# Decode attention on one core: one exp with eight masked copies, a product over half of K, and a whole third-last load

## The chip, the cores and the metric

One of the eight cores of a Trainium2 chip runs the whole kernel; the other cores are idle. The metric is the time of one execution on the device in microseconds, as a median of several runs. A sentence on names: PE is the matmul engine, DVE the vector engine, ACT the scalar engine, and SP the engine that only issues loads here.

Some words for reading the profiles. A page is the profiler's summary of one profiled run. A line of a timeline gives start and length in microseconds, engine, line of the kernel, operation, what it writes and reads, and how many instructions it sums up; brackets at its end give the time that the engine stood idle before it and what ended that. In a line of groups the numbers after the bar are busy microseconds and mean nanoseconds of one, then idle time before the group and what ended it. The granted clock is the share of PE's full speed that the trace's record of the clock gives for a stretch (1.0 or 0.5 in the profiles of both kernels). Slack is how much later a load could be issued without making the run longer.

## The reference

```python
B, H, Sq, Skv, Dh = 8, 32, 1, 4096, 128      # all bf16
def reference(q, k, v):
    scale = q.shape[-1] ** -0.5
    scores = jnp.einsum('bhqd,bhkd->bhqk', q, k) * scale
    attn = softmax(scores, axis=-1)
    return jnp.einsum('bhqk,bhkd->bhqd', attn, v)
```

There are 256 heads with one query each. K and V are 268 MB each and every byte is used once, so this is a kernel that streams memory.

## The kernel before

Eight heads make a tile: 128 partitions, 16 to a head, with 256 keys of 128 values on each partition. A tile of K or of V is one load of 8.39 MB. There are 32 tiles and three buffers of that size, which K and V share in turn.

DVE multiplies K by q and folds the 128 products of a key to 64 or 32; PE adds up further by multiplying with the identity; DVE finishes the sums to scores. One maximum per head follows, then ACT takes the exp. Eight copies of the weights are wanted, one per head, each nonzero only on that head's 16 partitions, since each value matmul takes the weights of all 128 partitions at once (`128*32` in the profile's lines):

```python
def product(t, lo, hi):
    kt = loads["k", t]
    qb = qbs[t]
    for c0 in range(lo, hi, MC):                     # MC = 64 keys, a quarter tile
        part = kt[:, c0 : c0 + MC, :]
        nc.vector.tensor_tensor(out=part, in0=part, in1=qb[:].to_broadcast([P, MC, D]), op=ALU.mult)
        nc.vector.tensor_tensor(out=part[:, :, 0 : D // 2], in0=part[:, :, 0 : D // 2],
                                in1=part[:, :, D // 2 : D], op=ALU.add)
        ...                                          # a second fold in some quarters
def weights_of(t):
    ...                                              # maximum of each head -> nmax
    nc.vector.tensor_scalar(out=bias[:], in0=own[:], scalar1=nmax[:, 0:1], ...)   # -1e30 for other heads
    for g in range(G):                               # G = 8
        nc.scalar.activation(out=w[:, :, g, :], in_=sc_g, func=ACT.Exp, bias=bias[:, g : g + 1],
                             scale=scale, accum_out=esum[:, t % R, g : g + 1])
```

The order of one turn, for the turns t = 1 to 29, in which a hardware loop does the value matmuls of tile t - 1:

```python
product(t, 0, Q);      sum_over_d(t, 0)              # Q = a quarter of the keys
...                                                  # result of tile t-2, q of tile t+2
product(t, Q, 2 * Q);  sum_over_d(t, 1);  scores_of(t, 0)
product(t, 2 * Q, 3 * Q);  sum_over_d(t, 2);  scores_of(t, 1)
...
product(t, 3 * Q, C);  sum_over_d(t, 3);  scores_of(t, 2)
values_loop(t - 1)                                   # 64 matmuls on PE
load("k", t + 1)                                     # waits for the value loop of tile t-2 to free its buffer
load("v", t)                                         # waits for PE's last sums of K of tile t
scores_of(t, 3);  weights_of(t);  ...
```

After the last tile PE does the values of tile 31 as the pieces of the last V come in: 32 matmuls on the first half, 30 on the later pieces, eight small ones for the last keys; then a copy, four matmuls, a scaling and the store.

Of the kernel before, what the change touches and what calls it, by code (L numbers as in the profile page):

```python
# [7 lines left out]
ACT = mybir.ActivationFunctionType  # L8
ALU = mybir.AluOpType
AX = mybir.AxisListType  # L10
BF16 = mybir.dt.bfloat16
F32 = mybir.dt.float32

G = 8
SLOTS = 3
TG = 4
R = 2
# [8 lines left out]
def kernel(  # L26
# [7 lines left out]
    nc = tc.nc  # L34
    B, H, Sq, D = q.shape
    S = k.shape[2]
    P = nc.NUM_PARTITIONS
    assert Sq == 1 and D == 128
    NH = B * H
    PH = P // G  # L40
    C = S // PH
    NT = NH // G
    scale = float(D) ** -0.5
    UC = 64
    DS = 512 // UC
    NU = C // UC
    MC = UC
    CB = 4
    RG = R * G
    NQ = NT // R  # L50
# [12 lines left out]
    consts = ctx.enter_context(tc.tile_pool(name="consts", bufs=1))  # L63
    q_pool = ctx.enter_context(tc.tile_pool(name="q_pool", bufs=3))
    w_pool = ctx.enter_context(tc.tile_pool(name="w_pool", bufs=2))
    sc_pool = ctx.enter_context(tc.tile_pool(name="sc_pool", bufs=2))
    small = ctx.enter_context(tc.tile_pool(name="small", bufs=2))
    o_pool = ctx.enter_context(tc.tile_pool(name="o_pool", bufs=1))
    ps_s = ctx.enter_context(tc.tile_pool(name="ps_s", bufs=3, space=bass.MemoryType.PSUM))
# [10 lines left out]
        out=ident[:], in_=ident[:], pattern=[[-1, P]], compare_op=ALU.not_equal,  # L80
        fill=1.0, base=0, channel_multiplier=1,
# [5 lines left out]
        out=heads[:], in_=heads[:], pattern=[[-1, G], [0, PH]], compare_op=ALU.not_equal,  # L87
        fill=1.0, base=0, channel_multiplier=1,
    )

    own = consts.tile([P, G], F32, name="own")
    nc.gpsimd.memset(own[:], 0.0)
    nc.gpsimd.affine_select(
        out=own[:], in_=own[:], pattern=[[-PH, G]], compare_op=ALU.is_ge,
        fill=NEG, base=0, channel_multiplier=1,
    )
    nc.gpsimd.affine_select(
        out=own[:], in_=own[:], pattern=[[PH, G]], compare_op=ALU.is_ge,
        fill=NEG, base=PH - 1, channel_multiplier=-1,
# [4 lines left out]
        out=same[:].rearrange("p (h x) -> p h x", x=PH),  # L104
        in_=own[:].rearrange("p (b h) -> p h b", h=TB // PH)
# [7 lines left out]
    for j in range(TG):  # L113
        part = pick[j * AG : (j + 1) * AG, :, :, :]
        nc.gpsimd.affine_select(
            out=part, in_=part, pattern=[[-1, CB], [CB * G, R], [-CB, RG]],
            compare_op=ALU.not_equal, fill=1.0, base=0, channel_multiplier=1,
        )
    ones = consts.tile([P, 1], F32, name="ones")
    nc.vector.memset(ones[:], 1.0)  # L120

    w_last = consts.tile([P, LAST, RG], BF16, name="w_last")
    nc.gpsimd.memset(w_last[:], 0.0)
# [4 lines left out]
    def behind_loop(made):  # L128
# [8 lines left out]

    cuts = {
        ("k", 0): [C // 4, C // 4, C // 2],
        ("k", NT - 3): [C // 2] * 2,  # L140
        ("k", NT - 2): [C // 2] * 2,
        ("k", NT - 1): [C // 4, C // 4, C // 2],
        ("v", NT - 1): [C // 2, C // 4, C // 8, C // 16, C // 32, LAST // 2, LAST // 2],
# [31 lines left out]
    def width_of(t, u):  # L175


        return D // 4 if u >= NU // 2 and 0 < t < NT - 3 else D // 2

    def product(t, lo, hi):  # L180
        kt = loads["k", t]
        qb = qbs[t]
        for c0 in range(lo, hi, MC):
            part = kt[:, c0 : c0 + MC, :]
            nc.vector.tensor_tensor(  # L185
                out=part, in0=part, in1=qb[:].to_broadcast([P, MC, D]), op=ALU.mult
            )
            nc.vector.tensor_tensor(  # L188
                out=part[:, :, 0 : D // 2], in0=part[:, :, 0 : D // 2],
                in1=part[:, :, D // 2 : D], op=ALU.add,  # L190
            )
            if width_of(t, c0 // UC) < D // 2:
                nc.vector.tensor_tensor(  # L193
                    out=part[:, :, 0 : D // 4], in0=part[:, :, 0 : D // 4],
                    in1=part[:, :, D // 4 : D // 2], op=ALU.add,
                )

    sums = {}

    def sum_over_d(t, u):  # L200
        kt = loads["k", t]
        ps = ps_s.tile([P, UC, DS], F32, name="ps", tag="ps")
        n = width_of(t, u) // DS
        for s in range(n):
            nc.tensor.matmul(  # L205
                ps[:], lhsT=ident[:],
                rhs=kt[:, u * UC : (u + 1) * UC, s * DS : (s + 1) * DS],
                start=(s == 0), stop=(s == n - 1),
            )
        sums[t, u] = ps  # L210
# [3 lines left out]
    def scores_of(t, u):  # L214
        if u == 0:
            scs[t] = sc_pool.tile([P, C], F32, name="sc", tag="sc")
        made = nc.vector.tensor_reduce(  # L217
            out=scs[t][:, u * UC : (u + 1) * UC], in_=sums.pop((t, u))[:], axis=AX.X, op=ALU.add
        )
        if u == NU - 1:  # L220
            behind_loop(made)

    ws = {}
    esums = {}

    def weights_of(t):
        sc = scs.pop(t)
        pmax = small.tile([P, 1], F32, name="pmax", tag="pmax")
        nc.vector.tensor_reduce(out=pmax[:], in_=sc[:], axis=AX.X, op=ALU.max)  # L229
        spread = small.tile([P, TB], F32, name="spread", tag="spread")  # L230
        nc.vector.tensor_scalar(
            out=spread[:], in0=same[:], scalar1=pmax[:, 0:1], scalar2=-scale,
            op0=ALU.add, op1=ALU.mult,
        )
        nmax = small.tile([P, 1], F32, name="nmax", tag="nmax")
        nc.vector.tensor_reduce(
            out=nmax[:], in_=spread[:], axis=AX.X, op=ALU.min, apply_transpose=True
        )
        bias = small.tile([P, G], F32, name="bias", tag="bias")
        nc.vector.tensor_scalar(  # L240
            out=bias[:], in0=own[:], scalar1=nmax[:, 0:1], scalar2=None, op0=ALU.add
        )
        w = w_pool.tile([P, C // CB, G, CB], BF16, name="w", tag="w")
        if t % R == 0:
            esums[t // R] = small.tile([P, R, G], F32, name="esum", tag="esum")
        esum = esums[t // R]
        sc_g = sc[:].rearrange("p (i m) -> p i m", m=CB)
        for g in range(G):
            nc.scalar.activation(  # L249
                out=w[:, :, g, :], in_=sc_g, func=ACT.Exp, bias=bias[:, g : g + 1], scale=scale,  # L250
                accum_out=esum[:, t % R, g : g + 1],
            )
        ws[t] = w
        if t == NT - 1:
            for i in range(LAST // CB):
                nc.gpsimd.tensor_copy(
                    out=w_last[:, i * CB : (i + 1) * CB, RG - G : RG].rearrange("p m g -> p g m"),
                    in_=w[:, (C - LAST) // CB + i, :, :],
                )
# [66 lines left out]

    def norm_of(n):
        zp = ps_z.tile([RG, 1], F32, name="zp", tag="zp")
        nc.tensor.matmul(
            zp[:], lhsT=esums.pop(n).rearrange("p r g -> p (r g)"), rhs=ones[:],  # L330
            start=True, stop=True,
        )
        zps[n] = zp

    def recip_of(n):
# [46 lines left out]
    Q = C // 4  # L382
# [3 lines left out]
    with tc.manual_schedule(engines={E.PE, E.DVE, E.Activation, E.SP}):  # L386
        q_prep(0)
        q_prep(1)
        for t in range(NT):
            loop = 0 < t <= LT  # L390
            v_last = t >= NT - 2
            n = t // R - 1
            if not loop:
                if t + 1 < NT:
                    load("k", t + 1)
                load("v", t)
            product(t, 0, Q)
            sum_over_d(t, 0)
            if 0 < t - 1 <= LT:
                if (t - 1) % R == 0:  # L400
                    norm_of(n)
                if t > 1:
                    result_of(t - 2)
            if t + 2 < NT:
                q_prep(t + 2)
            product(t, Q, 2 * Q)
            sum_over_d(t, 1)
            scores_of(t, 0)
            product(t, 2 * Q, 3 * Q)
            sum_over_d(t, 2)  # L410
            scores_of(t, 1)
            if t > 2 and t % R == 1:
                recip_of(n)
            product(t, 3 * Q, C)
            sum_over_d(t, 3)
            scores_of(t, 2)
            if loop:
                values_loop(t - 1)
                load("k", t + 1)
                load("v", t)  # L420
            if v_last:
                values_of(t - 1, 0, C)
            scores_of(t, 3)
            weights_of(t)
            if t > 2 and t % R == 1:
                finish_of(n)
            if t > 0:
                copy_of(t - 1)
                if t > 2 and t % R == 1:
                    store_of(n)  # L430
                if not loop:
                    if t % R == 0:
                        norm_of(n)
                    result_of(t - 1)
        values_of(NT - 1, 0, C // 2)
        norm_of(NQ - 1)
        recip_of(NQ - 1)
        values_of(NT - 1, C // 2, C - LAST)
        copy_of(NT - 1)
        result_of(NT - 1)  # L440
        finish_of(NQ - 1)
        store_of(NQ - 1)
# [30 lines left out]
```

## Time and profile before

| | before |
|---|---|
| time, median of 3 runs | 1252.86 us (1252.73 to 1252.98) |
| span in the profile | 1250.9 us |
| read from memory | 536.94 MB, 429 GB/s over the span |
| busy: PE, DVE, ACT | 62%, 83%, 14% |
| mean granted clock of PE | 0.787 |

The two things to look for are the throughput of the transfers, slice by slice, and what the last piece of work waited for. The prediction shows both. The row of PE's clock belongs beside them, as will turn out; here it is with the busy tenths of PE, from part 2 of the page of the kernel before, 40 slices of 31 us each:

```profile
PE   3465567755577555775557755577655776557756
PEclk9977788777887778877778777788777887778867
```

The clock granted to PE is not constant: 0.9 of full speed or more in two slices, 0.6 to 0.8 in the other 38.

### The profile page before, as it was taken

What the parts mean: (1) busy time and instruction counts of PE and PEld (TensorE: products, weight loads), DVE (VectorE), ACT (ScalarE), POOL (GpSimd) and SP (SyncE); (2) the same over time, 40 slices, a digit from 0 to 9 for tenths busy, and PEclk for the clock granted to TensorE, in tenths of its full rate; (3) what the DMA queues carried; (4) which work ended last, traced back from release to release, by engine and by line L of the source; (5) the groups of instructions that cost most, each with busy time, mean ns of one, the idle gap of its engine ahead of it and who ended that gap; (6) DMA issues with size and microseconds to landing.
All of it is one profiled execution on the core that took longest, in us unless ns stands there. A gap on an engine that the chain in (4) does not pass through costs nothing. (4 is left out here: it accounts for less than half of the span.)

```text
span 1250.9 us, 11080 instructions
## 1 busy us (share of the span) xinstructions
PE 770.4 (62%) x3078; PEld 289.4 (23%) x3078; DVE 1036.1 (83%) x586; ACT 170.7 (14%) x625; POOL 3.5 (0%) x19
## 2 busy tenths in 40 slices
PE   3465567755577555775557755577655776557756
PEld 1122122211222212222122221122221222122222
DVE  7887988888978889887798888988889887898783
ACT  0111011111011110111101111011110111101111
POOL 0000000000000000000000000000000000000000
PEclk9977788777887778877778777788777887778867
DMA  9999999999999999999999999999999999999997
GB/s 404 436 436 435 436 436 432 434 436 434 434 424 430 434 434 436 425 434 434 436 436 434 434 434 430 436 428 434 434 430 424 432 437 436 428 428 428 430 445 324
DMA packets 11577, 537.33 MB, mean 430 GB/s; under 512 B 1824, under 2 KB 2080, under 8 KB 2336
## 3 DMA queue, kind: packets, MB, share of 16 engines
q1 hardware_dynamic: 11216, 536.94, 99.4%
q8 instruction: 14, 0.23, 0.1%
q10 hardware_dynamic: 336, 0.07, 0.0%
q14 instruction: 11, 0.09, 0.0%
HBM read 536.94 MB, written 0.07 MB: 429 GB/s over the span
## 5 line engine op out<-in xcount | busy, mean ns | idle before, releaser
L185 DVE TENSOR_TENSOR kt<-kt,qb 128x8192 bf16<-128x8192 bf16 x128 | 565.3, 4416 | 127.9 <-DMA kt<-in_k_dram 103.5
L205 PE MATMUL ps<-kt,ident 128*128 128x512 bf16 x800 | 265.3, 483 | 432.4 <-DVE kt L193 366.8
L289 PE MATMUL av<-vt,w 128*32 x1740 | 426.1, 399 | 3.8
L188 DVE TENSOR_TENSOR kt<-kt 128x4096 bf16<-128x4096 bf16 x128 | 293.4, 2292 | 4.4
L289 PEld LDWEIGHTS av<-vt,w 128*32 x1740 | 174.4, 100 | 261.2 <-issue 114.4
L205 PEld LDWEIGHTS <-ident 128*128 128x128 bf16 x800 | 87.2, 113 | 597.0 <-issue 550.7
L249 ACT ACTIVATE w<-sc,bias 128x256 bf16<-128x256 f32 x256 | 126.3, 494 | 671.6 <-DVE bias L240 671.6
L217 DVE TENSOR_REDUCE sc<-ps 128x64 f32<-128x512 f32 x128 | 87.8, 686 | 57.3 <-PE ps L205 57.3
L193 DVE TENSOR_TENSOR kt<-kt 128x2048 bf16<-128x2048 bf16 x56 | 68.6, 1225 | 1.9
L345 ACT ACTIVATE comb<-av 32x512 bf16<-32x512 f32 (+1 forms) x32 | 18.8, 586 | 321.6 <-PEq L279 313.5
L275 PE MATMUL av<-vt,w 128*32 128x512 bf16 x116 | 47.1, 498 | 14.6 <-issue 13.4
L249 ACT ACTIVATION_READ_ACCUMULATOR w<-sc,bias 128x1 f32 x256 | 47.7, 187 | 0.0
L275 PEld LDWEIGHTS av<-vt,w 128*32 128x32 bf16 x116 | 6.9, 100 | 55.2 <-issue 55.2
L168 ACT ACTIVATE qg<-qh 8x128 bf16<-8x128 f32 x32 | 8.5, 267 | 73.8 <-PE qh L164 73.8
L317 PE MATMUL av<-vt,w 128*32 128x512 bf16 x190 | 14.7, 411 | 1.6 <-DMA vt<-in_v_dram 1.6
L361 PE MATMUL op<-comb,pick 32*16 32x128 bf16 (+1 forms) x128 | 12.3, 215 | 5.1 <-ACT comb L345 5.0
L229 DVE TENSOR_REDUCE pmax<-sc 128x1 f32<-128x256 f32 x32 | 13.4, 420 | 1.1
L170 PE MATMUL qp<-qg,heads 8*128 8x128 bf16 x32 | 6.9, 216 | 11.4 <-ACT qg L168 11.4
L164 PE MATMUL qh<-q_all,ident 128*8 128x128 bf16 x32 | 7.1, 223 | 8.7 <-DMA q_all<-in_q_dram 8.4
L172 ACT ACTIVATE qb<-qp 128x128 bf16<-128x128 f32 x32 | 8.9, 278 | 9.7 <-PE qp L170 9.7
L361 PEld LDWEIGHTS <-pick 32*16 32x16 bf16 (+1 forms) x128 | 6.8, 84 | 12.4 <-issue 12.0
L317 PEld LDWEIGHTS <-w 128*32 128x32 bf16 x190 | 6.5, 103 | 9.9 <-issue 5.5
(29 smaller groups left out, 47.4 us busy)
## 6 DMA issues: line engine op xcount, KB each, us to landing
kt<-in_k_dram SPq DMA_DIRECT2D x6, 4096.0 KB, 24.2
kt<-in_k_dram SPq DMA_DIRECT2D x4, 2048.0 KB, 13.4
vt<-in_v_dram SPq DMA_DIRECT2D x1, 4096.0 KB, 34.6
vt<-in_v_dram SPq DMA_DIRECT2D x1, 2048.0 KB, 39.1
vt<-in_v_dram SPq DMA_DIRECT2D x1, 1024.0 KB, 41.1
vt<-in_v_dram SPq DMA_DIRECT2D x1, 512.0 KB, 41.9
vt<-in_v_dram SPq DMA_DIRECT2D x31, 25.6
kt<-in_k_dram SPq DMA_DIRECT2D x28, 28.1
```

The source lines that it names most:

```text
L185: nc.vector.tensor_tensor(out=part, in0=part, in1=qb[:].to_broadcast([P, MC, D]), op=ALU.mult)
L188: nc.vector.tensor_tensor(out=part[:, :, 0 : D // 2], in0=part[:, :, 0 : D // 2], in1=part[:, :, D // 2 : D], op=ALU.add,)
L193: nc.vector.tensor_tensor(out=part[:, :, 0 : D // 4], in0=part[:, :, 0 : D // 4], in1=part[:, :, D // 4 : D // 2], op=ALU.add,)
L205: nc.tensor.matmul(ps[:], lhsT=ident[:], rhs=kt[:, u * UC : (u + 1) * UC, s * DS : (s + 1) * DS], start=(s == 0), stop=(s == n - 1),)
L217: made = nc.vector.tensor_reduce(out=scs[t][:, u * UC : (u + 1) * UC], in_=sums.pop((t, u))[:], axis=AX.X, op=ALU.add)
L229: nc.vector.tensor_reduce(out=pmax[:], in_=sc[:], axis=AX.X, op=ALU.max)
L249: nc.scalar.activation(out=w[:, :, g, :], in_=sc_g, func=ACT.Exp, bias=bias[:, g : g + 1], scale=scale, accum_out=esum[:, t % R, g : g + 1],)
L275: pe.matmul(av, lhsT=wf[:, i * nw : (i + 1) * nw], rhs=vf[:, i * nv : (i + 1) * nv], **how)
L289: pe.matmul(av, lhsT=wf[:, bass.ds(ow + i * nw, nw)], rhs=vf[:, bass.ds(ov + i * nv, nv)], start=False, stop=False,)
L317: nc.tensor.matmul(avs[t][j * AG : (j + 1) * AG, :], lhsT=w[:, i, :, :], rhs=vt[:, c0 : c0 + CB, :], start=(i < TG), stop=(j not in group[ ...
L345: nc.scalar.activation(out=comb[0:n, :, :], in_=av[0:n, :, :], func=ACT.Copy)
L361: nc.tensor.matmul(ops[n][:], lhsT=pick[0:e, m, r, :], rhs=comb[0:e, m, :], start=(r == 0 and m == 0), stop=(r == R - 1 and m == CB - 1),)
```

## The change

The change looks meant to save work on ACT and DVE. One exp per tile gives the weights once, and eight copies, each multiplied by a mask that is 1 on one head's partitions, spread them. In the turns 1 to 29 the first two quarters of K are multiplied in one instruction. The third-last K comes in one load instead of two. The diff is cut: the scores' buffers also go from two to one, together with the one exp.

```diff
+    mine = consts.tile([P, R, RG], F32, name="mine")      # 1 where partition and head belong together
...
-        ("k", NT - 3): [C // 2] * 2,
...
-        for c0 in range(lo, hi, MC):
-            part = kt[:, c0 : c0 + MC, :]
+        part = kt[:, lo:hi, :]
...
-        bias = small.tile([P, G], F32, name="bias", tag="bias")
-        nc.vector.tensor_scalar(out=bias[:], in0=own[:], scalar1=nmax[:, 0:1], scalar2=None, op0=ALU.add)
+        e = o_pool.tile([P, C], BF16, name="e", tag="e")
+        nc.scalar.activation(out=e[:], in_=sc[:], func=ACT.Exp, bias=nmax[:, 0:1], scale=scale,
+                             accum_out=esums[t // R][:, t % R : t % R + 1])
         for g in range(G):
             nc.scalar.activation(
-                out=w[:, :, g, :], in_=sc_g, func=ACT.Exp, bias=bias[:, g : g + 1], scale=scale,
-                accum_out=esum[:, t % R, g : g + 1],
+                out=w[:, :, g, :], in_=e_g, func=ACT.Copy, scale=mine[:, 0, g : g + 1]
             )
...
-            product(t, 0, Q)
-            sum_over_d(t, 0)
+            product(t, 0, 2 * Q if loop else Q)
+            if not loop:
+                sum_over_d(t, 0)
...                                                    # in turns 1 to 29: sums 0 and 1 together,
...                                                    # scores 0 and 1 together after the third quarter
```

The normalisation changes with it. Before, each of the eight copies brought its own sum of weights, and one matmul for a pair of tiles added them up. Now there is one sum per partition and tile, and two small matmuls with the mask add them up by head.

More of the change, by code (lines that the diff above doesn't have):

```diff
@@ L46 @@
     NU = C // UC
-    MC = UC
     CB = 4
@@ L65 @@
     w_pool = ctx.enter_context(tc.tile_pool(name="w_pool", bufs=2))
-    sc_pool = ctx.enter_context(tc.tile_pool(name="sc_pool", bufs=2))
+    sc_pool = ctx.enter_context(tc.tile_pool(name="sc_pool", bufs=1))
     small = ctx.enter_context(tc.tile_pool(name="small", bufs=2))
@@ L118 @@
         )
-    ones = consts.tile([P, 1], F32, name="ones")
-    nc.vector.memset(ones[:], 1.0)
+    mine = consts.tile([P, R, RG], F32, name="mine")
+    nc.gpsimd.memset(mine[:], 1.0)
+    nc.gpsimd.affine_select(
+        out=mine[:], in_=mine[:], pattern=[[PH * G, R], [-PH, RG]], compare_op=ALU.is_ge,
+        fill=0.0, base=0, channel_multiplier=1,
+    )
+    nc.gpsimd.affine_select(
+        out=mine[:], in_=mine[:], pattern=[[-PH * G, R], [PH, RG]], compare_op=ALU.is_ge,
+        fill=0.0, base=PH - 1, channel_multiplier=-1,
+    )
     w_last = consts.tile([P, LAST, RG], BF16, name="w_last")
@@ L182, in product @@
         qb = qbs[t]
-        for c0 in range(lo, hi, MC):
-            part = kt[:, c0 : c0 + MC, :]
+        part = kt[:, lo:hi, :]
+        nc.vector.tensor_tensor(
+            out=part, in0=part, in1=qb[:].to_broadcast([P, hi - lo, D]), op=ALU.mult
+        )
+        nc.vector.tensor_tensor(
+            out=part[:, :, 0 : D // 2], in0=part[:, :, 0 : D // 2],
+            in1=part[:, :, D // 2 : D], op=ALU.add,
+        )
+        if width_of(t, lo // UC) < D // 2:
             nc.vector.tensor_tensor(
-                out=part, in0=part, in1=qb[:].to_broadcast([P, MC, D]), op=ALU.mult
-            )
-            nc.vector.tensor_tensor(
-                out=part[:, :, 0 : D // 2], in0=part[:, :, 0 : D // 2],
-                in1=part[:, :, D // 2 : D], op=ALU.add,
-            )
-            if width_of(t, c0 // UC) < D // 2:
-                nc.vector.tensor_tensor(
-                    out=part[:, :, 0 : D // 4], in0=part[:, :, 0 : D // 4],
-                    in1=part[:, :, D // 4 : D // 2], op=ALU.add,
-                )
+                out=part[:, :, 0 : D // 4], in0=part[:, :, 0 : D // 4],
+                in1=part[:, :, D // 4 : D // 2], op=ALU.add,
+            )
     sums = {}
@@ L238, in weights_of @@
         )
-        bias = small.tile([P, G], F32, name="bias", tag="bias")
-        nc.vector.tensor_scalar(
-            out=bias[:], in0=own[:], scalar1=nmax[:, 0:1], scalar2=None, op0=ALU.add
+        if t % R == 0:
+            esums[t // R] = small.tile([P, R], F32, name="esum", tag="esum")
+        e = o_pool.tile([P, C], BF16, name="e", tag="e")
+        nc.scalar.activation(
+            out=e[:], in_=sc[:], func=ACT.Exp, bias=nmax[:, 0:1], scale=scale,
+            accum_out=esums[t // R][:, t % R : t % R + 1],
         )
         w = w_pool.tile([P, C // CB, G, CB], BF16, name="w", tag="w")
-        if t % R == 0:
-            esums[t // R] = small.tile([P, R, G], F32, name="esum", tag="esum")
-        esum = esums[t // R]
-        sc_g = sc[:].rearrange("p (i m) -> p i m", m=CB)
+        e_g = e[:].rearrange("p (i m) -> p i m", m=CB)
         for g in range(G):
             nc.scalar.activation(
-                out=w[:, :, g, :], in_=sc_g, func=ACT.Exp, bias=bias[:, g : g + 1], scale=scale,
-                accum_out=esum[:, t % R, g : g + 1],
+                out=w[:, :, g, :], in_=e_g, func=ACT.Copy, scale=mine[:, 0, g : g + 1]
             )
@@ L328, in norm_of @@
         zp = ps_z.tile([RG, 1], F32, name="zp", tag="zp")
-        nc.tensor.matmul(
-            zp[:], lhsT=esums.pop(n).rearrange("p r g -> p (r g)"), rhs=ones[:],
-            start=True, stop=True,
-        )
+        esum = esums.pop(n)
+        for r in range(R):
+            nc.tensor.matmul(
+                zp[:], lhsT=mine[:, r, :], rhs=esum[:, r : r + 1], start=(r == 0), stop=(r == R - 1)
+            )
         zps[n] = zp
@@ L405 @@
                 q_prep(t + 2)
-            product(t, Q, 2 * Q)
+            if loop:
+                sum_over_d(t, 0)
+            else:
+                product(t, Q, 2 * Q)
             sum_over_d(t, 1)
-            scores_of(t, 0)
+            if not loop:
+                scores_of(t, 0)
             product(t, 2 * Q, 3 * Q)
             sum_over_d(t, 2)
+            if loop:
+                scores_of(t, 0)
             scores_of(t, 1)
```

## The prediction

> **What bounds the kernel now.** I read the page's busy line first, then its row of DMA throughput, then the chain that ended last, then the queue of loads (times of issue and of landing), and last the timeline of one tile.
>
> The page, parts 1 to 3:
>
> ```profile
> PE 770.4 (62%) x3078; PEld 289.4 (23%) x3078; DVE 1036.1 (83%) x586; ACT 170.7 (14%) x625; POOL 3.5 (0%) x19
> ...
> DMA  9999999999999999999999999999999999999997
> GB/s 404 436 436 435 436 436 432 434 436 434 434 424 430 434 434 436 425 434 434 436 436 434 434 434 430 436 428 434 434 430 424 432 437 436 428 428 428 430 445 324
> ...
> HBM read 536.94 MB, written 0.07 MB: 429 GB/s over the span
> ```
>
> No compute engine is full; the transfers are, in every slice but the first and the last. No slice of the middle falls below 424 or stays above 436 GB/s. At 436 the 536.94 MB take 1231.5 us; the span is 1250.9, so everything that isn't transfer at that rate is 19.4 us, 1.6%. A change that leaves the bytes alone cannot gain 2% (25 us) here.
>
> The chain of work that ended last:
>
> ```profile
> DMA 3%; DVE 1%; PE 1%; SPq 0%; ACT 0%; issue 0%; DVEq 0%; ACTq 0%
> ...
> 1204.53 41.99 DMA vt<-in_v_dram
> 1246.53 0.04 issue
> 1246.57 0.41 PE av L317 x2
> ```
>
> The chain is cut short at the left, but its end is clear: the last pieces of the last V were issued at 1204.53 and landed 42 us later, because two other loads stood before them. After the landing come two matmuls, a copy, four matmuls, a scaling and the store: some 4.4 us to 1250.9.
>
> Whether the queue of loads ever runs dry is read from part 6 of the page and from the timeline of the issuing engine:
>
> ```profile
> vt<-in_v_dram SPq DMA_DIRECT2D x31, 25.6
> kt<-in_k_dram SPq DMA_DIRECT2D x28, 28.1
> ...
> 441.52 0.33 SPq L151 DMA_DIRECT2D kt<-in_k_dram  x1
> 463.58 0.33 SPq L151 DMA_DIRECT2D vt<-in_v_dram  x1
> 480.53 0.33 SPq L151 DMA_DIRECT2D kt<-in_k_dram  x1
> ```
>
> A whole load is 8.39 MB and takes 19.2 us at 436 GB/s. V lands 25.6 us after issue and K 28.1. Take off the moving and 1.3 us of fixed latency (the 4 KB store at the end landed in 1.3), and a V load has stood in the queue for 5.1 us, a K load for 7.6. So each could be issued that much later before the transfers would notice. Issues come 38.7 us apart for a pair, two times 19.2 and a little.
>
> The vector engine waits for K, not the other way round (timeline of one tile):
>
> ```profile
> 463.98 1.04 PE L275 MATMUL av<-vt,w 128*32 128x512 bf16 x2 [0.43 <-issue]
> ...
> 469.75 4.43 DVE L185 TENSOR_TENSOR kt<-kt,qb 128x8192 bf16<-128x8192 bf16 x1 [4.23 <-DMA kt<-in_k_dram]
> ...
> 474.21 2.29 DVE L188 TENSOR_TENSOR kt<-kt 128x4096 bf16<-128x4096 bf16 x1
> ...
> 476.43 4.42 DVE L185 TENSOR_TENSOR kt<-kt,qb 128x8192 bf16<-128x8192 bf16 x1
> ```
>
> DVE starts the tile when K has landed, after 4.23 us of waiting, and 32.4 us later (502.15) the sums are out and the next V is issued. DVE's spare time per tile is thus about 4.3 of 38.7 us. The value loop starts at 463.98 and its end at 480.4 lets the K load go.
>
> [...] 8192 elements 4416 ns, 4096 elements 2292, 2048 elements 1225, thus 0.52 ns an element and 150 to 160 ns fixed. [...]
>
> **The change part by part.** The name speaks of six value matmuls per loop turn, but the loop constant is 6 in both kernels; nothing changes there. The bytes stay the same.
>
> *One exp, eight copies.* Out go 256 exps (126.3 us busy), 256 accumulator reads (47.7) and 32 bias additions on DVE (7.4 us). In come 32 exps (32 x 0.494 = 15.8), 32 reads (6.0) and 256 copies with a pointer scale[...]. ACT busy falls to about 145 us. Per tile, the time from maximum to finished weights: before, eight steps of 0.49 (465.56, 466.06, 466.55), 4.0 us in all. After: the exp, its read and a wait for its output, 0.7[...]. The weights of tile t are used only a tile later, so this lies beside other work except in the last tile. The normalisation gets one more tiny accumulating matmul per pair of tiles, 16 times some 0.2 us on PE, off the path.
>
> *Two quarters in one product.* In the 29 loop tiles two multiplications of 8192 become one of 16384: 8.53 + 0.15 = 8.7 instead of 8.83 us, and the addition likewise 4.42 instead of 4.58. Saved: 0.15 twice, 0.3 us a tile. The first score reduction (0.68) moves behind the third quarter; its length stays. So the last sums, hence V's issue, come 0.3 us earlier relative to K's landing. DVE busy falls by 29 x 0.3 + 7.4 = 16 us, to about 1020, and its wait for K grows by 0.5 us a tile. The first 16 sum matmuls start after both quarters, about 13.1 us after landing (say 482.8) instead of at the loop's end (480.5). PE waits there, and has nothing that sets an end.
>
> *Third-last K whole.* Before, DVE began tile 29 at 1126.21, on the first half. Whole, it starts by the rhythm: 1091.92 + 38.7 = 1130.6, or 4.4 us later. But before, DVE then stood 3.65 us at the first score reduction, until PE had left the value loop; with the reduction moved, that wait goes. After: 1130.6 + 13.05 (both quarters) + 6.7 + 1.3 (two reductions) + 0.1 + 6.7 + 3.6 (last sums) = 1162.0, against V's issue at 1161.59. The shift is +0.4 us, against 5 of slack. Tiles 30 and 31 keep their order and are shifted by 0.2 to 0.4. The last weights are ready at 1238.3 instead of 1238.05; PE then still waits for V (1.09 us at 1242.24, 0.2 before the last two matmuls), so the shift is swallowed.
>
> Sum on the path: start of transfers 0, transfers 0 [...], tail after the last landing 0. The result is **1252.6 us**, 0.3 below the median of before.
>
> **Rivals.** *A dry queue:* the shift in tile 29 exceeds the slack, or V1 at the start is issued too late (75.42, where K2's transfer ends near 79). For it: the slack is smallest there. Against it: the shift is 0.4, and V1 moves earlier by 0.3. If I missed the removed wait, 4.4 us of shift would still be inside 5.1; a spill would make 1253 to 1256. *Faster transfers:* pairs take 38.8 us, not 38.5 as at 436 GB/s; if that loss came from the engines' traffic in SBUF, fewer instructions could give back part of 19 us, thus 1245 to 1250. Against it: stretches of 38.7 us each, tile after tile, read 429 to 434 GB/s (one 426), whatever the tile does, and I find no dip that belongs to an engine's work. *ACT as a bound:* with copies twice as dear as I think, weights come 4 us later; loop tiles have over 30 us to spare, but in the last tile half of V is waiting and PE would take the place of the landing; 1254 to 1256. *A slower clock on PE:* the loop takes 16.4 us and ends 7.6 before K's queue is dry, so even 25% would pass.
>
> **Range and chances.** The three runs of before lie within 0.25 us, and nothing on the path is touched, so I take 1251.2 to 1254.0 for 8 in 10: a little for small changes in how transfers meet, and for the tail. Faster by 2% would need more than the ceiling allows: 0.01. Slower by 2% needs a dry queue in nearly every tile: 0.01. Within 2%: 0.98.
>
> **What would show it right or wrong.** Right: the row of GB/s still at 434, landing times about 25.9 and 28, DVE busy near 1020, ACT near 145, the product of 16384 at 8.7 us, no wait for the first score in tile 29, the chain again ending in V's landing. Wrong: a slice of GB/s under 420 in the middle or near tile 29, landing times near 20.5, copies at 0.9 us, or a last chain that runs through ACT's copies instead of the landing.

The sum on the path came to 0 + 0 + 0, so 1252.6 us. ACT's 145 us came from 170.7 - 126.3 - 47.7 + 15.8 + 6.0 + 126: the 126 stands for 256 copies at 0.49 us each, my estimate, by which a copy takes as long as an exp (494 ns on the page). The time from maximum to weights came to 0.7 + 3.3 = 4.0 us after the change, thus no change, less 0.23 for the bias addition; the 3.3 for eight copies (seven steps of 0.40 and a last 0.49), an estimate too, is cut with the sum. In the trace of the kernel before, 0.40 us pass from the start of an exp to the start of its read (466.06 to 466.46). The times for 8192, 4096 and 2048 elements are those of DVE's operations in lines 185, 188 and 193 of the kernel before. "The ceiling" is the 436 GB/s of that page's slices, which I took as a bound; experiment 8 measures the loads alone, 1245.78 us.

## The result, and the profile after

The changed kernel took 1252.36 us, median of 6 runs (1251.73 to 1253.11); the kernel before, on the same chip, 1252.86 (1252.73 to 1252.99, 6 runs). The ratio is 0.9996, with a 95% interval of 0.9983 to 1.0009: the same. A ratio here is the mean time of one kernel's fast runs over that of the other's of the same rounds, so it is not quite the ratio of the medians.

The median hides something. The six runs were 1251.73, 1251.77, 1251.81 and 1252.91, 1253.00, 1253.11: two groups 1.2 us apart, and the kernel before has one group only. The profiled run is of the slower group. Its page, parts 1 to 3:

```profile
PE 794.4 (63%) x3110; PEld 301.4 (24%) x3110; DVE 1021.8 (82%) x495; ACT 166.1 (13%) x433; POOL 4.1 (0%) x22
...
DMA  9999999999999999999999999999999999999997
GB/s 404 436 436 434 436 436 432 434 436 432 432 426 430 437 434 434 430 430 436 436 436 434 434 434 432 432 430 436 434 432 432 430 435 436 436 434 418 430 437 318
```

The row of throughput is the old one but for a few dips. The deepest, 418 in slice 37 (1126 to 1157 us, where tile 29 is), lies just under the 420 that the prediction had named as a sign of being wrong. It was no dry queue: by the packet records at least 16 packets were in hand at every moment from 1110 to 1180 us. DVE gave back 14 us (1036.1 to 1021.8), ACT 5, and PE shows 24 us more of busy time. None of it shows in the time.

The costs of the single operations, from the groups of the changed kernel with shapes kept apart:

```profile
L191 DVE TENSOR_TENSOR kt<-kt,qb 128x16384 bf16<-128x16384 bf16 x29 | 252.0, 8691 | 139.7 <-DMA kt<-in_k_dram 139.7
...
L255 ACT ACTIVATE w<-e,mine 128x256 bf16<-128x256 bf16 x256 | 105.6, 495 | 1.1
...
L248 ACT ACTIVATE e<-sc,nmax 128x256 bf16<-128x256 f32 x32 | 16.2, 508 | 705.9 <-DVE nmax L242 705.9
```

The merged product takes 8.69 us, as worked out. DVE stood idle before the multiplications of K for 146.7 us in all (the multiplications by one quarter, not shown, included), against 127.9 in the kernel before. That is 19 us more: what DVE saved, and a little more, it waits for.

The queue of loads, part 6 of the page of the changed kernel (the last number is the microseconds from issue to landing):

```profile
vt<-in_v_dram SPq DMA_DIRECT2D x31, 25.9
kt<-in_k_dram SPq DMA_DIRECT2D x29, 28.4
```

Both stand 0.3 us longer in the queue than before (25.6 and 28.1), because they are issued 0.3 us sooner and land when they did.

What ended the run is new. The chain of work that ended last, in the profiled run of the changed kernel (start, length, what):

```profile
1201.87 39.43 DMA vt<-in_v_dram
1241.30 0.04 issue
1241.35 5.93 PE av L322 x26
1247.28 0.02 issue
```

Before, the chain's last wait was for a landing at 1246.53. Now it is a landing at 1241.30, and from there on PE works through 5.9 us without waiting for anything: PE ends the run, not the transfer. The timeline of PE in that stretch of the two kernels shows why. Before:

```profile
1239.01 0.27 PE L361 MATMUL op<-comb,pick 128*16 128x128 bf16 x2 [2.50 <-ACT comb L345]
...
1239.23 1.89 PE L317 MATMUL av<-vt,w 128*32 128x512 bf16 x29
...
1242.24 3.40 PE L317 MATMUL av<-vt,w 128*32 128x512 bf16 x24 [1.09 <-DMA vt<-in_v_dram]
...
1246.57 0.39 PE L317 MATMUL av<-vt,w 128*32 128x512 bf16 x2 [0.20 <-DMA vt<-in_v_dram]
```

After:

```profile
1237.62 0.27 PE L367 MATMUL op<-comb,pick 128*16 128x128 bf16 x2 [2.53 <-ACT comb L351]
...
1237.84 2.72 PE L322 MATMUL av<-vt,w 128*32 128x512 bf16 x29
...
1241.35 5.91 PE L322 MATMUL av<-vt,w 128*32 128x512 bf16 x30 [0.71 <-DMA vt<-in_v_dram]
```

The same 29 matmuls take 2.72 us instead of 1.89. The clock tells the rest. Stretches of the changed kernel, PE alone (length, busy time, granted clock, share of DMA, GB/s):

```profile
1238.00:1239.00 1.00, 1.00 (x24) 0.88 1.09 459
1239.00:1245.00 6.00, 5.29 (x26) 0.50 0.78 312
1245.00:1246.00 1.00, 1.00 (x13) 0.71 0.11 39
```

The clock is halved from about 1238.8 to 1245.6 (0.88 and 0.71 of a microsecond's mean say where inside it the switch lies). In the kernel before all three stretches read 1.00. The bytes, meanwhile, were early: only 39 GB/s flow between 1245 and 1246, where the kernel before still moved 77. (By its packet records, 16 packets are in hand there until about 1243.0 us, and only one from 1246.0.)

### The profile page after: what moved, and what is told of

Its sections match the earlier page's. It is cut to its first block, busy times and chain, and to the rows that moved or that the text cites. A ratio compares the mean times of both kernels' runs of the same rounds, so it can differ in the third digit from the quotient of the medians.

```text
span 1251.1 us, 10828 instructions
## 1 busy us (share of the span) xinstructions
PE 794.4 (63%) x3110; PEld 301.4 (24%) x3110; DVE 1021.8 (82%) x495; ACT 166.1 (13%) x433; POOL 4.1 (0%) x22
## 3 DMA queue, kind: packets, MB, share of 16 engines
q1 hardware_dynamic: 11072, 536.94, 99.4%
## 5 line engine op out<-in xcount | busy, mean ns | idle before, releaser
L191 DVE TENSOR_TENSOR kt<-kt,qb 128x8192 bf16<-128x8192 bf16 (+1 forms) x99 | 560.8, 5665 | 146.7 <-DMA kt<-in_k_dram 139.7
L211 PE MATMUL ps<-kt,ident 128*128 128x512 bf16 x800 | 284.1, 519 | 383.5 <-DVE kt L199 295.2
L194 DVE TENSOR_TENSOR kt<-kt 128x4096 bf16<-128x4096 bf16 (+1 forms) x99 | 288.8, 2917 | 3.4
L211 PEld LDWEIGHTS <-ident 128*128 128x128 bf16 x800 | 97.0, 121 | 563.9 <-issue 530.0
L248 ACT ACTIVATE e<-sc,nmax 128x256 bf16<-128x256 f32 x32 | 16.2, 508 | 705.9 <-DVE nmax L242 705.9
L255 ACT ACTIVATE w<-e,mine 128x256 bf16<-128x256 bf16 x256 | 105.6, 495 | 1.1
## 6 DMA issues: line engine op xcount, KB each, us to landing
vt<-in_v_dram SPq DMA_DIRECT2D x31, 25.9
kt<-in_k_dram SPq DMA_DIRECT2D x29, 28.4
```

Source lines behind the costliest of these rows:

```text
L211: nc.tensor.matmul(ps[:], lhsT=ident[:], rhs=kt[:, u * UC : (u + 1) * UC, s * DS : (s + 1) * DS], start=(s == 0), stop=(s == n - 1),)
L248: nc.scalar.activation(out=e[:], in_=sc[:], func=ACT.Exp, bias=nmax[:, 0:1], scale=scale, accum_out=esums[t // R][:, t % R : t % R + 1],)
L255: nc.scalar.activation(out=w[:, :, g, :], in_=e_g, func=ACT.Copy, scale=mine[:, 0, g : g + 1])
```

## The experiments

The theory: the end of the run is set by whichever comes later, the last bytes of V or PE's work on them; all that the change saves or adds in the 1230 us before that is taken up by waits for the transfers. The rivals: the three parts have gains and losses that cancel by chance; or the half microsecond is noise.

**1. The kernel before, again.** Nothing edited.

> The kernel before, unchanged, against itself. It shows how far two sets of runs of one kernel stand apart and whether its times fall in one group. If the half microsecond between the two kernels is chance, the runs spread over more than the 0.25 us that six runs showed; if the kernel before has one group only, all runs are again within 1252.7 to 1253.0 and the ratio is 1.0000 within 0.0002.

Measured: 1252.72 us (1252.50 to 1252.80, 5 runs) against 1252.69 (1252.58 to 1252.91, 9 runs), ratio 1.0000. Two runs, 1252.50 and 1252.57, lie a little below what I expected. The kernel before has one group, about half a microsecond wide when all sets are put together. The two groups of the changed kernel are therefore its own. In the profiled run here PE's clock did fall for a while: the 29 matmuls took 2.78 us, and the last 30 took 4.72 from 1242.10 on without a wait. The run still took 1252.50, since the bytes come late enough in this kernel that PE is done with them at about the same time.

So the clock can fall in the kernel before too. In the clock records of the first profiles of the two kernels the clock is granted in full or in half, and each of the 67 and 117 stretches between two changes lasts a whole multiple of 3.41 us (3.41 to 27.3 us); near the end the half stretch is 3.4 us in this run, 6.8 in the changed kernel. Next, the one stretch of 3.41 us into which most of PE's wait for the last weights falls (length, busy time of PE, granted clock, share of DMA, GB/s): in the first profile of the kernel before, in the changed kernel and in this run.

```profile
1237.11:1240.53 3.42, 1.52 (x32) 1.00 0.95 398
...
1235.35:1238.76 3.41, 1.14 (x24) 1.00 0.96 406
...
1236.59:1240.00 3.41, 1.06 (x23) 1.00 0.97 404
```

PE was busy for 44%, 33% and 31% of them. The clock stayed full after the first and fell after the other two. The waits themselves are 2.50, 2.53 and 2.72 us; of the first 1.90 lie inside the stretch, of the second 2.27. Where these stretches begin is not the same in two profiles of one kernel (1237.11 and 1236.59). So the length of the wait alone does not part these three; where it falls in the stretches may. In experiments 3, 5 and 6 the clock fell after stretches with PE busy for 11%, 24% and 11%. In experiments 2, 4, 7, 9 and 10, where it stayed, PE's longest wait near the end was 2.29, 0.38, 0.55, 0.30 and 0.68 us. No share of busy time that would keep the clock up is shown: over the whole profile of the changed kernel it fell after stretches of 3.41 us with PE busy for 0% to 70%, and stayed after one with 45%.

**2. The third-last K whole, alone.**

```diff
-        ("k", NT - 3): [C // 2] * 2,
```

> The kernel before with the third-last K loaded whole, and nothing else. Theory of slack: DVE starts that tile about 4.4 us later (near 1130.5), but the loop's sums hold it back less, V of that tile is issued 1 to 4.4 us later (1162.5 to 1166), which is inside the 5 us that a V load stands in the queue, so the time stays within 1252.5 to 1253.5. Rival, a dry queue: the shift passes the slack, a dip in throughput shows near 1170, and the time rises by 1 to 4 us. Rival, the whole load is what brings the last V home 0.8 us earlier in the changed kernel: here too the last landing comes near 1245.7 and the time is near 1252.0.

Measured: 1252.87 us (1252.77 to 1253.00), ratio 1.0002. The timeline of DVE has that tile start at 1130.95 instead of 1126.07 (in the run of experiment 1), after a wait for the load:

```profile
1130.95 4.42 DVE L184 TENSOR_TENSOR kt<-kt,qb 128x8192 bf16<-128x8192 bf16 x1 [4.37 <-DMA kt<-in_k_dram]
...
1144.28 0.68 DVE L216 TENSOR_REDUCE sc<-ps 128x64 f32<-128x512 f32 x1
1144.88 4.41 DVE L184 TENSOR_TENSOR kt<-kt,qb 128x8192 bf16<-128x8192 bf16 x1
```

The first score reduction at 1144.28 has no wait, where the kernel before waits 3.65 us. So of 4.9 us, V's issue gets 1.1 (1162.59 against 1161.47), and the time gets nothing. The landing did not come sooner either (PE's last wait ended at 1246.85), so this part is not what brings the bytes home early.

**3. The changed kernel without that part.** The line of experiment 2 put back into the changed kernel.

> The changed kernel with the third-last K again in two halves. Theory: that part alone moves nothing; two groups of times remain, near 1251.8 and near 1253.0, as in the changed kernel. If the whole load is the cause of the earlier last landing, the group near 1251.8 is gone and all runs lie near 1252.8.

Measured: 1252.35 us, with runs of 1251.70, 1251.84, 1252.35, 1252.42 and 1253.09; ratio 0.9995. The spread stays, from 1251.7 to 1253.1, now with two runs between the groups. Both directions agree: the third part does nothing to the time. The profiled run, 1253.09, again has the clock at half (its last 30 matmuls take 5.79 us). The totals hide something here. Without the whole load, V of tile 29 is issued at 1156.69 and the last maximum comes at 1228.47; in the changed kernel these are 1160.80 and 1232.60. So with the merged product the whole load gives back 4.1 us of lead, which the time does not feel.

**4. The changed kernel with PE kept at work near the end.** Sixty matmuls into a tile that nobody reads, where PE waits anyway.

```diff
+    def keep_warm(n):
+        hot = ps_q.tile([P, D], F32, name="hot", tag="qp")
+        for i in range(n):
+            nc.tensor.matmul(hot[:], lhsT=ident[:], rhs=q_all[:, 0, :], start=True, stop=True)
...
                 values_of(t - 1, 0, C)
+                if t == NT - 1:
+                    keep_warm(40)
...
         norm_of(NQ - 1)
+        keep_warm(20)
```

> The changed kernel with 60 matmuls whose result is not used, in the two waits of PE near the end (40 after the values of tile 30, 20 after the last normalisation). Theory: the changed kernel's two groups come from PE's clock in the last 10 us, which in its profiled run fell to half from 1239 to 1245.6 so that PE and not the landing ended the run; with PE kept at work the clock is granted in full, PE waits for each last piece, and all runs lie in the faster group, 1251.5 to 1252.0. Rival, the two groups come from the landing of the last V: then they remain, 1251.8 and 1253.0.

Measured: 1251.82 us (1251.60 to 1251.95, 5 runs), ratio 0.9993, interval 0.9979 to 1.0007. The interval holds 1, but all of these runs are faster than the fastest of the kernel before. The slower group is gone. The timeline of PE in that run:

```profile
1234.90 2.41 PE L391 MATMUL hot<-q_all,ident 128*128 128x128 bf16 x40
...
1237.68 1.89 PE L322 MATMUL av<-vt,w 128*32 128x512 bf16 x29
...
1241.25 3.40 PE L322 MATMUL av<-vt,w 128*32 128x512 bf16 x24 [0.38 <-DMA vt<-in_v_dram]
...
1245.61 0.39 PE L322 MATMUL av<-vt,w 128*32 128x512 bf16 x2 [0.25 <-DMA vt<-in_v_dram]
```

The 29 and the 24 take the same 1.89 and 3.40 us as in the kernel before, PE waits for each last piece, and the last wait ends at 1245.61, 0.96 us before that of the kernel before (1246.57). That explains the two groups: with the clock full the run ends with the bytes, near 1251.8; with the clock halved it ends with PE, near 1253.0. (Of the changed kernel itself only a run of the slower group was profiled; that its faster runs had the full clock is inferred from this experiment, not seen.) This is also the fastest version.

**5. The one exp and the eight copies, alone in the kernel before.** The edit is the middle part of the change, with the normalisation and the single buffer of scores that go with it.

> The kernel before with the one exp and the eight masked copies alone. Theory of slack: ACT busy falls by about 5 us, the last weights are ready some 0.5 us sooner, nothing on the path changes; 1252.2 to 1253.0 with one or two groups. If this part is what brings the last bytes home 0.8 us sooner (fewer instructions, so fewer fetches of instructions between the data packets), the faster group near 1251.8 shows up, with the last data packet ending near 1245.9.

Measured: 1253.63 us (1253.45 to 1254.91, 5 runs), ratio 1.0006 against 1252.81. This was outside what I expected, and on the wrong side. The timeline of PE (profiled run, 1254.91 us):

```profile
1237.24 0.38 PE L369 MATMUL op<-comb,pick 128*16 128x128 bf16 x4 [2.67 <-ACT comb L353]
...
1242.45 6.71 PE L324 MATMUL av<-vt,w 128*32 128x512 bf16 x30 [1.74 <-DMA vt<-in_v_dram]
```

The weights are ready sooner, PE does the first half sooner, waits 1.74 us for V, and takes 6.71 us for its last 30. The clock is 0.50 to 0.51 from 1238 to 1246.

**6. The merged product, alone in the kernel before** (with its order; K of tile 29 in halves, eight exps).

> The kernel before with the merged product and its order alone (third-last K in halves, eight exps). Theory of slack: 1252.3 to 1253.0; V is issued 0.3 us sooner each tile, DVE waits 0.3 us longer for K. If this part is what brings the last bytes home sooner, the faster group near 1251.8 shows up here and not with the one exp alone.

Measured: 1253.59 us (1253.19 to 1253.99, 5 runs), ratio 1.0007. Again slower than expected, and again PE's last 30 matmuls run without a further wait, 5.30 us, from a start at 1242.27 (1.32 us of waiting before it); the 32 before them take 3.61 us, against 1.91 in experiment 10. The last exp ends 4.9 us sooner than in the kernel before (1233.2 against 1238.1), PE waits 2.88 us for the first half of V, and the clock is half from 1235.0 to 1245.2.

**7. The kernel before with PE kept at work.** The edit of experiment 4.

> The kernel before with the same 60 unused matmuls in PE's last waits. Theory: before, the end is set by the last bytes (landing near 1246.6) whatever PE's clock, so keeping the clock up gains at most 0.2 us: 1252.4 to 1252.8. Rival, the clock alone is what parts the two kernels' faster groups: then it comes down to 1251.8 like the changed kernel with its tail kept warm.

Measured: 1252.67 us (1252.61 to 1252.86), ratio 1.0000. The clock alone gives the kernel before nothing: its last wait is for the bytes (ended at 1246.53).

**8. The loads alone.** All computation taken out; the result is wrong (zeros).

```diff
+    for t in range(NT):
+        if t + 1 < NT:
+            load("k", t + 1)
+        load("v", t)
```

> Wrong result on purpose (zeros): all loads of the changed kernel, in the same order and into the same three buffers, and no computation; only a store of zeros. It measures the floor that the transfers set. Each 64 KB packet took 2.42 us on its engine and each engine moves 512 of them, 1239 us. Theory of slack: the kernel is within the tail after the last landing (4.4 us) and a little of that floor, so this one takes 1244 to 1248. Rival, the waits for computation leave holes between the transfers: then it falls well below, under 1240.

Measured: 1245.78 us (1245.66 to 1246.28, 4 runs), ratio 0.9945. So loads of this size, in this order and into these three buffers, leave the computation at most 7.0 us (0.6%) to gain; and some 4.4 of the 7.0 us are the tail after the last landing.

**9 and 10. Each part alone, with PE kept at work.** Experiments 5 and 6 with 72 and 120 unused matmuls in PE's last waits.

> The one exp alone in the kernel before, as in the run that took 1253.6, plus 40 and 32 unused matmuls in PE's last two waits. Theory: that run's 0.8 us over the kernel before came from PE's clock alone: its weights are ready sooner, PE then waits longer for the last V (1.74 us), falls to half clock and takes 6.7 us instead of 4.7 for the last 30 value matmuls. With the clock kept up the time is 1251.6 to 1252.8 and the last 24 take 3.4 us. Rival: the part itself delays the landing (last data packet 1247.0 in that run); then 1253.0 and more remain.

> The merged product alone in the kernel before, as in the run that took 1253.6, plus 40, 40 and 40 unused matmuls in PE's three last waits. Theory of the clock, as for the one exp: 1251.6 to 1252.8. Rival, a late landing (last data packet 1246.8 in that run): 1253.0 and more remain.

Measured: 1252.86 us (1252.65 to 1252.99) for the one exp, ratio 1.0001; 1252.72 us (1252.63 to 1253.00) for the merged product, ratio 1.0000. The 0.8 us that each part alone had lost are gone. So the loss went with PE's clock. But neither part falls to the 1251.8 of experiment 4. The last wait of PE in the timeline of experiment 9:

```profile
1246.62 0.39 PE L324 MATMUL av<-vt,w 128*32 128x512 bf16 x2 [0.22 <-DMA vt<-in_v_dram]
```

And in that of experiment 10:

```profile
1246.77 0.39 PE L316 MATMUL av<-vt,w 128*32 128x512 bf16 x2 [0.26 <-DMA vt<-in_v_dram]
```

The bytes come home at 1246.6 to 1246.8, as in the kernel before, and 1.0 us later than with both parts together.

**11. How much slack is there: one more DVE operation per tile.** A maximum of a quarter of K with itself, so the result stays right.

```diff
+        if lo == 0 and 0 < t < LT:
+            for c0 in (0,):                       # (0, UC) in experiment 12
+                more = kt[:, c0 : c0 + UC, :]
+                nc.vector.tensor_tensor(out=more, in0=more, in1=more, op=ALU.max)
```

> The changed kernel with one more DVE operation of 128 x 8192 (a maximum of K with itself, so the result stays right) at the start of tiles 1 to 28: 4.42 us of DVE work more per tile, 124 us in all. Theory of slack: DVE's wait for K (4.88 us) shrinks to about 0.5, V is issued 4.4 us later, its time to landing falls from 25.9 to about 21.5, and the time stays within 1251.7 to 1253.5. Rival, DVE or V's issue is on the path: then up to 124 us are added.

Measured: 1285.77 us (1283.70 to 1294.98, 4 runs), ratio 1.0282. A miss. I expected 4.4 us a tile to vanish in 5.1 of slack; of 28 x 4.42 = 124 us, 33 came through, 1.2 us a tile. The page shows where:

```profile
GB/s 425 427 425 423 419 429 411 410 414 427 427 411 408 427 420 425 406 416 421 429 423 417 402 423 425 445 403 425 394 443 433 396 425 397 425 450 405 430 443 332
```

The transfers run short in many slices, while DVE still waits 1.8 to 2.6 us for K in the tiles that I looked at. DVE is not full; my reading is that the loads are issued too late. By the delay the slack is 4.42 - 1.2 = 3.2 us, not 5.1; the runs spread over 11 us, so this is rough. It doesn't all fit: V's time from issue to landing fell only to 24.1 us (I expected 21.5), which leaves some 2 us of queue by the measure of experiment 12. That the added operation slows the transfers in some other way was not tested apart.

**12. Two more operations per tile.**

> The same with two such operations, 8.84 us more per tile. Theory of slack: the tile's DVE time (33.8 us from start to the next start if K is there) becomes 42.6, more than the 38.7 of the two loads, so each of 28 tiles takes 3.9 us longer: about 1362 us (1350 to 1375), DVE waits no more for K, and throughput falls to about 394 GB/s. Rival, there is more slack than I count: the time rises by less than 80 us.

Measured: 1358.49 us (1358.10 to 1358.73, 4 runs), ratio 1.0843. As expected: DVE now goes from tile to tile without a wait for K, one tile takes 42.5 us (V is issued at 466.52 and, two tiles on, at 551.59), and throughput over these two tiles is 395 GB/s. It also gives the missing number, part 6 of its page:

```profile
vt<-in_v_dram SPq DMA_DIRECT2D x31, 22.0
```

Here a V load finds the queue empty: V was issued at 466.52, and K had been issued at 440.90 with 24.6 us to landing, which is 465.5. A load that waits for no other then takes 22.0 us here, not 19.2 + 1.3. So in the changed kernel a V load stands at most 25.9 - 22.0 = 3.9 us in the queue, which is near the 3.2 found by delay.

## Why the prediction was right or wrong, point by point

- **What bounds the kernel** was right: experiment 8 shows that the loads alone take 99.4% of the time. The time predicted was 1252.6, measured 1252.36, and the ratio is within noise of 1, as forecast. The signs named for it mostly came: landing times of 25.9 and 28.4, DVE near 1020, no wait for the first score in tile 29. Two did not: ACT's busy time, and the last chain, which in the profiled run does not end in V's landing.
- **The merged product** was right: 8.69 us against 8.7. From DVE's start to V's issue the changed kernel takes 32.14 us (469.84 to 501.98), before 32.40; 0.26 saved, 0.3 predicted. DVE busy is 1021.8 against about 1020.
- **The cost of the copies** was right: 0.495 us each, where 0.49 was estimated; and from the start of the exp to the end of the copies 3.9 us in the last tile (1232.91 to 1236.84; the eight copies take 3.30), where 4.0 was estimated. **ACT busy near 145 us** was wrong: 166.1. I took the summed durations of exps and accumulator reads away from the engine's total, but neighbours overlap (in the kernel before, the exp of 465.56 ends at 466.07 and its read starts at 465.97); those two groups alone sum to 174.0 us (126.3 and 47.7), more than the engine's 170.7 in all. By the time per tile, which I had, the saving had to be near nothing, and it is 5 us of 170.
- **The third-last K** was right in its mechanism: the wait for the first score is gone, and V's issue moves 1.1 us later with this part alone (experiment 2). Its size with the merged product was not: there the part moves V's issue 4.1 us later (1156.69 in experiment 3, 1160.80 in the changed kernel), since without it V is issued 4.9 us sooner than in the kernel before (1161.59). Against the kernel before, both together bring V's issue 0.8 us sooner (1160.80 against 1161.59), where 0.4 later was predicted.
- **The slack of 5.1 us** was mis-sized: 3.2 by delay (experiment 11), 25.6 - 22.0 = 3.6 by landing times (experiment 12). The term that failed is the fixed latency of 1.3 us, taken from a 4 KB store; a whole load with an empty queue lands 2.8 us after its moving time (22.0 - 19.2). It did no harm, since the shift was at most 1.1 us (experiment 2). My remark that even 4.4 us of shift would pass did not hold in experiment 11, where every tile had it.
- **The tail, "the shift is swallowed"**, is the step that failed inside a right total. I expected weights at 1238.3; they came at 1236.8, sooner than before (the last maximum alone came 1.1 us sooner, 1232.60 against 1233.68). And I gave no thought to what PE's clock does near the end: in the changed kernel's profile it is halved from 1238.8 to 1245.6, and PE ends after the bytes. I had named a slower clock as a rival, but looked only at the value loop, where there is room. That the clock is the cause is shown by keeping PE at work: parts alone 1253.6, kept at work 1252.7 to 1252.9; both parts 1251.7 to 1253.1, kept at work 1251.6 to 1252.0. That the clock fell in the changed kernel because the weights came sooner is not shown: its two waits are not longer than before (2.53 against 2.50 us, 0.71 against 1.09), and the fall also came in the unchanged kernel (experiment 1, after 2.72 us). Longer waits stood in the parts alone (1.74 and 2.88 us) and in experiment 3 (2.87). That it depends on where a wait falls is a reading of the stretches under experiment 1, not tested apart.
- **The last bytes, 0.8 to 1.0 us sooner** with both parts together, I did not foresee. The three kernels that have both parts and no added delay show it, those with one part or none do not: by the packet records the last data packet ends at 1245.8 to 1246.2 in the changed kernel and experiments 3 and 4, at 1246.6 to 1247.0 in the kernel before and experiments 1, 2, 5, 6, 7, 9 and 10. The third-last K is ruled out as its cause by experiments 2 and 3. That neither other part does it alone is not so firm, for the runs were made on three chips: the changed kernel and experiments 1 to 4 on one, 5 to 8 on a second, 9 to 12 on a third. No kernel with both parts and a normal queue ran on the other two, and neither of these parts ran alone on the first. (The kernel before takes 1252.7 to 1252.8 on all three.) One candidate, fewer transfers of instructions between the data, isn't borne out: 11 and 14 such packets in the kernel before on its two instruction queues, 9 and 15 in the changed one. Each kernel has one profile. The cause stays open.

So the gain of a tail with sooner bytes (about 0.9 us) and the loss from the halved clock (about 1.2 us, in half of the runs, thus 0.6 on average) partly cancel. Each is at most 0.1% of the time. The prediction knew of neither; that its time lies 0.24 us from the measured median is to that extent luck.

## What to carry to other kernels

In this kernel, whose loads stream almost without a break (the loads alone take 99.4% of the time), work saved elsewhere turned into waiting (DVE: 14 us less work, 19 us more waiting for K); measure the floor with the loads alone before tuning instructions. Measure the slack of a queue by delaying it (3.2 us here, where 5.1 was worked out), or take its latency from a load of the same size (2.8 us beyond the moving time), not from a small one (1.3 us). Where PE waits for the last data, look at its clock: here it fell to half in some runs, which cost about 1.2 us; a few unused matmuls in the wait made the runs agree, and with the change they gave 0.07%, in an interval that holds zero.
